# Loading r through GpSimd's queue from unit 8 on, in an RWKV-attention and squared-ReLU kernel with a planned order

## Chip, core and metric

The kernel runs on one core of one Trainium2 chip. The metric is device time in microseconds, of the whole launch. Before the change three runs gave a median of 180.85 us (178.78 to 181.63).

## What is computed

Two stages follow each other. The first is a linear attention with decay: per batch (4), head (8) and step (768), with head size 48,

```python
for t in range(S):
    cur = np.einsum('bhd,bhe->bhde', u[None] * kt, vt)
    y[:, :, t] = np.einsum('bhd,bhde->bhe', rt, state + cur)
    state = w[None, :, :, None] * state + np.einsum('bhd,bhe->bhde', kt, vt)
```

The second takes y as 3,072 tokens of 384 numbers and computes `relu(x @ w_in) ** 2 @ w_out`, with 2,048 numbers between the two products. Inputs and output are float32.

## The kernel before

**Units.** The sequence is cut into 6 chunks of 128 steps. A unit is one chunk of one batch with all 8 heads: 24 units, chunk by chunk, four batches in each. A unit has three loads of 192 KB, `rt`, `kt` and `vt` (`load`, L294); a row of such a load is one head of one step, 192 bytes long.

**Attention of a unit.** VectorE scales r and k by powers of w into `rkw` (L315). `rkw` is transposed into `rkT`: for the first six units on TensorE (L335) with evictions on ScalarE (L339), from then on by a DMA transpose (L324). TensorE multiplies the two halves of `rkT` (`at`, L352), VectorE applies the causal mask (L364) and multiplies the halves (`rk`, L344); `sums` (L372, L377) gives the diagonal term and the chunk's addition to the state; `dv` (L386) is VectorE's, the state is updated on VectorE (L394 to L400) and cast on ScalarE (L406). ScalarE casts v to `vb` (L319). `y` is summed on TensorE (L415 from the masked products, L421 from the state), `yb` is evicted on VectorE (L430), and turned into `xT` on TensorE for six units (L446), by a DMA transpose after that (L439).

**Second stage of a unit.** `mm1` (L462) multiplies with `w_in`, in four steps a unit, one for each quarter of `w_in`; the first eight units go alone (128 columns), the other sixteen in pairs (256 columns). ScalarE takes the ReLU out of PSUM (L470), and ScalarE (L477) or VectorE (L479) squares it into `g`, five to three. `mm2` (L486) multiplies `g` with the four quarters of `w_out` one after the other, `osb` is evicted on ScalarE (L493) and stored (L520). The last unit's second layer is cut in two column parts (L501, L510, L512, L516).

**Queues.** SyncE issues all loads, all stores and all DMA transposes, in its own program order. GpSimd issues the eight quarters of the weights (L303, L306), each after a one-element copy out of some unit's k (`gate`, L300), which keeps that weight behind this load. Both stand idle until what the next instruction on them waits for is there.

**The order.** Nothing is scheduled by the compiler: `Plan` holds every step with its engine, an estimated cost, what it needs, which buffers it takes and a rank, and `Plan.run` plays a list schedule through. Each engine takes the step with the lowest rank among those that are ready and whose buffers and PSUM banks are free; the order that comes out is the program order of that engine. For DMAs it keeps a model of each queue: at most about 1.5 us of work may be waiting, and queues that move at once share the rate. Fillers (`fill`, L262) are matmuls on a constant with the highest ranks, so they land in TensorE's planned waits, nearly all of them in the start.

Of the kernel before, what the change touches and what calls it, by code (L numbers as in the profile page):

```python
# [15 lines left out]

class Plan:

    def __init__(self, lags, cold):
        self.lags = lags
        self.cold = cold
        self.steps = []  # L30
        self.at = {}
        self.users = {}
        self.place = {}

    def add(self, key, engine, cost, emit, needs=(), rank=0.0, new=(), uses=(), move=None, cold=None):
        s = dict(key=key, engine=engine, cost=cost, emit=emit, rank=rank, new=new, move=move, cold=cold)
        s["needs"] = [n for n in needs if n is not None]
        self.at[key] = s
        self.steps.append(s)
        for x in tuple(new) + tuple(uses):  # L40
            self.users.setdefault(x, []).append(s)

    def run(self, room, banks, count):
        todo = {}
        for s in self.steps:
            todo.setdefault(s["engine"], []).append(s)
        for mine in todo.values():
            mine.sort(key=lambda s: s["rank"])
        rings = {name: [] for name in room}
        free = {e: 0.0 for e in todo}  # L50
        queues = {e: [] for e in todo}
        held = {n: None for n in range(count)}
        since = {n: 0.0 for n in range(count)}
        order = []
        t = 0.0
        left = len(self.steps)
        tiny = 1e-9

        moved, chained, left_pe, to_pe, near = self.lags

        def ready(s, e):
            if s["move"]:
                return s["end"] + moved
            if s["engine"] == "PE":
                return s["end"] + (chained if e == "PE" else left_pe)
            return s["end"] + (to_pe if e == "PE" else near)

        marks = []

        def mark(s):  # L70
            for e in ("PE", ""):
                heappush(marks, ready(s, e))

        def done(s, e):
            return "end" in s and ready(s, e) <= t + tiny

        def fits(s):
            e = s["engine"]
            names = [x[0] for x in s["new"]]
            for name in set(names):  # L80
# [3 lines left out]
                for n in range(len(ring) - m, len(ring) - m + names.count(name)):  # L84
                    if n >= 0 and not all(done(x, e) for x in self.users[ring[n]]):
                        return False
            wanted = [name for name in names if name in banks]
            if wanted:
                for n, x in held.items():
                    if x is not None and all(done(u, e) for u in self.users[x]):  # L90
                        held[n], since[n] = None, max(u["end"] for u in self.users[x])
                if sum(x is None for x in held.values()) < len(wanted):
                    return False
                for name in set(wanted):
                    mine = sum(x is not None and x[0] == name for x in held.values())
                    if mine + wanted.count(name) > banks[name]:
                        return False
            return True

        while left:  # L100
            for e, mine in todo.items():
                if free[e] > t + tiny:
                    continue
                for s in mine:
                    if s["move"] and sum(x[1] / x[0]["move"][0] * x[0]["move"][3] for x in queues[e]) > 1.5:
                        continue
                    if all(done(self.at[k], e) for k in s["needs"]) and fits(s):
                        mine.remove(s)
                        left -= 1
                        for x in s["new"]:  # L110
                            if x[0] in banks:
                                n = min((n for n in held if held[n] is None), key=lambda n: since[n])
                                held[n] = x
                                self.place[x] = n
# [4 lines left out]
                        if s["move"]:  # L119
                            queues[e].append([s, s["move"][0], free[e] + s["move"][2]])  # L120
                        else:
                            s["end"] = free[e]
                            mark(s)
                        order.append(s)
                        break
            heads = [q[0] for q in queues.values() if q]
            moving = [x for x in heads if x[2] <= t + tiny]
            whole = sum(x[0]["move"][1] for x in moving)
# [4 lines left out]
            later += [x[2] for x in heads if x[2] > t + tiny]  # L133
            later += [t + x[1] * whole / x[0]["move"][1] for x in moving]
            if not later:
                if left:
                    raise ValueError("nothing can go on: " + str([s["key"] for m in todo.values() for s in m[:3]]))
                break
            step = min(later) - t
            t += step  # L140
            for x in moving:
                x[1] -= step * x[0]["move"][1] / whole
                if x[1] <= 1e-7:
                    queues[x[0]["engine"]].pop(0)
                    x[0]["end"] = t
                    mark(x[0])
        return order
# [3 lines left out]
def kernel(  # L151
# [21 lines left out]
    NPE = 6  # L173
    NPY = 6
    NPAD = 5
    SQUARES = 'AMAMAAAM'
    GROUPS = (1,) * 8 + (2,) * 8
    PAIRED = ()

    const = ctx.enter_context(tc.tile_pool(name="const", bufs=1))  # L180
    loads = ctx.enter_context(tc.tile_pool(name="loads", bufs=6))
# [535 lines left out]
```

## Time and profile before

| what | value |
|---|---|
| three runs, median (lowest, highest) | 180.85 us (178.78, 181.63) |
| span of the profiled execution (clock granted 0.999) | 178.1 us |
| the profiled execution's own time beside its span | none is listed; the lowest run is 0.7 us over the span |
| TensorE busy | 169.5 us, of which fillers 12.5 |
| VectorE, ScalarE, GpSimd busy | 129.5, 128.4, 13.1 us |
| first `mm1`, last matmul's end | 15.1 us, 175.2 us |
| loads to landing, median: r, k, v | 3.6, 4.2, 4.1 us |
| stores; transposes rkT, xT; weights `w_in`, `w_out` | 2.4; 3.8, 3.0; 7.2, 10.1 us |

A row of a group gives line, engine, operation, tiles, the count, then the busy time, the mean in ns of one, the idle time before them and what ended most of it. Matmuls overlap in the pipeline, so TensorE's busy time is more than the sum of what each adds; what one adds is read from the chain of work that ended last, where pieces follow each other without overlap. A stretch's row gives its length and each engine's busy time in it.

### The profile page before, as it was taken

The page shows a single profiled execution, that of the slowest core. Times are in us where ns is not written, and L with a number is a line of the kernel's source. Part 1 is how long each engine was busy: PE and PEld are TensorE (multiplying, and loading weights), DVE is VectorE, ACT ScalarE, POOL GpSimd, SP SyncE. Part 2 cuts the span into 40 slices and gives each one's busy share as a digit, 9 for nine tenths or more (in the row PEclk, how much of TensorE's full clock was granted, in tenths as well). Part 3 has the DMA queues.
Part 4 walks back from the last instruction along what each step waited for, and adds up shares of the span by engine and source line. Part 5 has one row for each costly group of instructions (what it writes and reads, how often), then busy time and mean ns, then how long its engine had stood idle before and what let it go on. Part 6 is the DMA issues. An engine that isn't in the chain of part 4 may idle for free.

```text
span 178.1 us, 4985 instructions
## 1 busy us (share of the span) xinstructions
PE 169.5 (95%) x2013; PEld 134.9 (76%) x2013; DVE 129.5 (73%) x282; ACT 128.4 (72%) x266; POOL 13.1 (7%) x40
## 2 busy tenths in 40 slices
PE   7999799999999999999899899999999999999993
PEld 4778698987787786795696596786786885887972
DVE  4589697294999989689699598788798595771310
ACT  4556789999487984597598299498399494693941
POOL 6280650000000000000000000000000000000000
PEclk9999999999999999999999999999999999999999
DMA  6999899996595979879799999899999989953012
GB/s 115 188 182 204 156 198 199 207 184 109 84 207 118 184 140 171 175 152 207 159 175 192 155 180 151 189 178 141 200 201 151 192 184 161 262 177 110 0 48 88
DMA packets 107241, 28.84 MB, mean 162 GB/s; under 512 B 101969, under 2 KB 106706, under 8 KB 107218
## 3 DMA queue, kind: packets, MB, share of 16 engines
q1 hardware_dynamic: 104976, 25.37, 77.2%
q0 software_dynamic: 2240, 3.15, 9.8%
q8 instruction: 15, 0.25, 0.6%
q14 instruction: 8, 0.07, 0.1%
q10 hardware_dynamic: 2, 0.00, 0.0%
HBM read 20.45 MB, written 4.72 MB: 141 GB/s over the span
## 4 chain that ended last, share of the span: by engine, by line
PE 58%; DMA 21%; DVE 11%; ACT 4%; issue 1%; SPq 1%; POOL 1%; DVEq 0%; ACTq 0%
PE bank L462 26%; PE bank L486 20%; DMA rkT<-rkw 6%; DMA rt<-in_r_dram 5%; DMA w_in_q<-in_moe_w_in_dram 5%; PE bank L352 3%; DVE am L364 2%; DVE rkw L315 2%; DMA xT<-yb 2%; DVE g L479 2%; ACT gr L470 2%; DVE yb L430 2%; DMA vt<-in_v_dram 2%; PE bank L415 2%; PE bank L501 1%
## 5 line engine op out<-in xcount | busy, mean ns | idle before, releaser
L462 PE MATMUL bank<-xT,w_in_q 128*128 128x128 bf16 (+1 forms) x768 | 73.1, 246 | 2.0 <-DMA w_in_q<-in_moe_w_in_dram 1.3
L462 PEld LDWEIGHTS <-w_in_q 128*128 128x128 bf16 x768 | 62.4, 114 | 5.1 <-DMA w_in_q<-in_moe_w_in_dram 1.6
L486 PE MATMUL bank<-w_out_q,g 128*128 128x384 bf16 x368 | 64.7, 326 | 0.0
L470 ACT ACTIVATE gr<-bank 128x512 f32<-128x512 f32 x96 | 53.7, 594 | 10.3 <-PE bank L462 10.0
L486 PEld LDWEIGHTS <-g 128*128 128x128 bf16 x368 | 34.8, 98 | 20.2 <-DVE g L479 0.2
L479 DVE TENSOR_TENSOR g<-gr 128x512 bf16<-128x512 f32 x36 | 24.7, 687 | 19.5 <-ACT gr L470 19.5
L477 ACT ACTIVATE g<-gr 128x512 bf16<-128x512 f32 x60 | 37.0, 635 | 0.8
L364 DVE TENSOR_TENSOR am<-bank,smask 128x512 bf16<-128x512 f32 x48 | 31.6, 686 | 4.0 <-PE bank L352 3.6
L319 ACT CAST vb<-vt 128x384 bf16<-128x384 f32 x24 | 12.4, 515 | 15.4 <-DMA vt<-in_v_dram 15.3
L406 ACT CAST stb<-st 64x192 bf16<-64x192 f32 x40 | 14.0, 349 | 5.4 <-DVE st L400 4.3
L315 DVE TENSOR_TENSOR rkw<-kt,wneg 128x384 bf16<-128x384 f32 x24 | 13.3, 554 | 5.4 <-DMA kt<-in_k_dram 5.3
L315 DVE TENSOR_TENSOR rkw<-rt,wpos 128x384 bf16<-128x384 f32 x24 | 13.3, 552 | 3.8 <-ACT wpos L269 2.4
L430 DVE TENSOR_TENSOR yb<-bank,dv 128x384 bf16<-128x384 f32 x24 | 13.4, 557 | 2.3 <-PE bank L421 1.8
L493 ACT COPY osb<-bank 128x384 f32<-128x384 f32 x23 | 11.2, 486 | 5.3 <-PE bank L486 5.2
L344 DVE TENSOR_TENSOR rk<-rkT 128x512 bf16<-128x512 bf16 x24 | 10.1, 422 | 5.0 <-DMA rkT<-rkw 5.0
L262 PE MATMUL bank<-warm 128*128 128x128 bf16 x135 | 12.5, 244 | 1.1 <-DVE warm L209 1.1
L386 DVE TENSOR_TENSOR dv<-vb,bank 128x384 f32<-128x384 bf16 x24 | 13.1, 546 | 0.5 <-PE bank L377 0.4
L262 PEld LDWEIGHTS <-warm 128*128 128x128 bf16 x135 | 9.9, 111 | 2.3 <-issue 1.1
L396 DVE TENSOR_TENSOR st<-bank,st 64x192 f32<-64x192 f32 x32 | 11.3, 352 | 0.2
L352 PE MATMUL bank<-rkT 64*128 64x128 bf16 x192 | 9.7, 222 | 0.9 <-DMA rkT<-rkw 0.9
L352 PEld LDWEIGHTS <-rkT 64*128 64x128 bf16 x192 | 5.5, 95 | 6.4 <-issue 2.9
L415 PEld LDWEIGHTS <-am 128*128 128x128 bf16 x192 | 8.2, 96 | 1.9 <-DVE am L364 0.6
(57 smaller groups left out, 101.6 us busy)
## 6 DMA issues: line engine op xcount, KB each, us to landing
rt<-in_r_dram SPq DMA_DIRECT2D x24, 192.0 KB, 3.6
kt<-in_k_dram SPq DMA_DIRECT2D x24, 192.0 KB, 4.2
vt<-in_v_dram SPq DMA_DIRECT2D x24, 192.0 KB, 4.1
out_dram<-osb SPq DMA_DIRECT2D x23, 192.0 KB, 2.4
w_in_q<-in_moe_w_in_dram POOLq DMA_DIRECT2D x4, 384.0 KB, 7.2
w_out_q<-in_moe_w_out_dram POOLq DMA_DIRECT2D x4, 384.0 KB, 10.1
rkT<-rkw SPq DMA_TRANSPOSE x18, 3.8
xT<-yb SPq DMA_TRANSPOSE x18, 3.0
```

The lines of the kernel that those rows point to most:

```text
L262: nc.tensor.matmul(out=bank("fill")[:, :128], lhsT=warm, rhs=warm, start=True, stop=True)
L315: nc.vector.tensor_tensor(t["rkw"][:, x, :, :, :D], pair(src), pair(wx), ALU.mult)
L352: nc.tensor.matmul(out=t["at"][o][:, p, :], lhsT=t["rkT"][sl, 1, p, :], rhs=t["rkT"][sl, 0, p, :], start=True, stop=True,)
L364: nc.vector.tensor_tensor(am, t["at"][o], smask.unsqueeze(1).to_broadcast([C, HP, C]), ALU.mult)
L386: nc.vector.tensor_tensor(t["dv"], t["vb"], t["d"].unsqueeze(2).to_broadcast([C, H, D]), ALU.mult)
L406: nc.scalar.copy(stb[b][sl, :, o * D : (o + 1) * D], st32[b][sl])
L430: nc.vector.tensor_tensor(t["yb"], t["y"], t["dv"].rearrange("p h d -> p (h d)"), ALU.add)
L462: nc.tensor.matmul(out=t["h", s][:, a], lhsT=turned, rhs=chunks[c]["xT"][:, n, b : b + m, :], start=(n == 0), stop=(n == NK - 1),)
L470: nc.scalar.activation(t["gr", s], t["h", s], AF.Relu)
L477: nc.scalar.activation(g, x, AF.Square)
L479: nc.vector.tensor_tensor(g, x, x, ALU.mult)
L486: nc.tensor.matmul(out=t["o"], lhsT=chunks[units[i][0]]["g"][:, f, units[i][1], :], rhs=w_out_q[f // 4][:, f % 4, :], start=(f == 0), stop ...
```

## The change

r's loads from unit 8 on, and all stores but those of the last three units, are issued by GpSimd. k, v and the transposes stay on SyncE, and so does r of units 0 to 7. An r load on GpSimd needs, in the plan, that the r load three units earlier has landed.

All of the plan's settings move into one dictionary. The planner's DMA model is replaced: a move has a duration and a delay, two queues that move at once go at 0.62 each unless said otherwise, and instruction fetches are modelled as a stop of 2 us each time a count of planned PE instructions is passed (294 first, then every 246), in which GpSimd's queue goes at 0.85, SyncE's loads at 0.1 and its transposes not at all. Ranks of nearly all steps are new, and they can lie far from the unit's place.

Weights: the order by rank and the load that each is held behind are new. r, k and v get buffers of their own (4, 5, 4) in place of six of each, and other counts change too: rkT 3 for 4, vb 8 for 4, the masked products 6 for 4 each, yb 3 for 4, gr 10 for 8, osb 9 for 8, padded rkw tiles 4 for 5. The caps on PSUM banks by use rise (s 3, y 4, o 6), out of the same eight banks. The fillers are 68 of 256 columns in place of 135 of 128. Of eight squares, five stay on ScalarE in another pattern.

```diff
+P = {'squares': 'AAMAMAAM',
+ 'wide': 256,
+ 'fills': 68,
+ 'fetch': (294, 246, 2.0, (0.85, 0.0, 0.1)),
+ 'front': ('U0', 'U1', 'U2', 'U3', 'U4'),
+ 'weights': ('O0', 'I0', 'O1', 'O2', 'O3', 'I1', 'I2', 'I3'),
+ 'gates': {'I0': ('vt', 1), 'I1': ('kt', 3), 'I2': ('vt', 5), 'O0': ('vt', 3),
+           'I3': ('rt', 3), 'O1': ('kt', 4), 'O2': ('rt', 1), 'O3': ('rt', 2)},
+ 'rank': {'load': 72.19, 'vload': 7.28, 'scale': -0.67, 'rkT': 41.16, 'xT': 54.94, 'out': 43.52,
...
+ 'stores': 'POOL',
+ 'soft': ('rt',),
+ 'softfrom': 8,
+ 'depth': {'SP': 1.55},
...
     def load(i, name):
-        x = loads.tile([C, H, D], F32, name=name)
-        nc.sync.dma_start(
+        x = buffer({"rt": "ldr", "kt": "ldk", "vt": "ldv"}[name], [C, H, D], F32)
+        (nc.gpsimd if i >= P["softfrom"] and name in P["soft"] else nc.sync).dma_start(
...
-    def weights(i, q, which):
-        nc.gpsimd.tensor_copy(gate, tiles[i]["kt"][:, 0, :1])
+    def weights(after, q, which):
+        if after is not None:
+            nc.gpsimd.tensor_copy(gate, tiles[after[1]][after[0]][:, 0, :1])
...
-    def store(i):
-        nc.sync.dma_start(out=out[b * S + c * C : b * S + (c + 1) * C, :], in_=tiles[i]["osb"])
+    def store(i, where):
+        (nc.gpsimd if where == "POOL" else nc.sync).dma_start(out=..., in_=tiles[i]["osb"])
...
-    front = ['U0', 'U1', 'I0', 'I1', 'U2', 'U3', 'I2', 'O0', 'U4', 'I3', 'O1', 'O2', 'O3', 'U5']
...
+            hard = i < P["softfrom"] or name not in P["soft"]
             copy(
-                (name, i), SP, 0.55, do(load, i, name), rank=rank + 0.1 * n, move=(1.06, 16, 0.67, 1.0),
-                new=[("ld", i)] if n == 0 else (), uses=[("ld", i)] if n else (),
+                (name, i), SP if hard else POOL, 0.43 if hard else 1.2, do(load, i, name), rank=rank + 0.1 * n + (R["vload"] if n == 2 and i >= 6 else 0), move=moves["load"],
+                needs=[] if hard else [(name, i - 3)], new=[("ld" + name[0], i)],
             )
...
-                copy(("out", j), SP, 0.42, do(store, j), rank=a + 4 + L2, needs=[("osb", j)], move=(0.58, 75, 0.67, 0.13), uses=[("osb", j)])
+                where = P["stores"] if j < NU - 3 else SP
+                copy(
+                    ("out", j), where, 0.42 if where == SP else 0.7, do(store, j, where), rank=a + 4 + L2 + R["out"],
+                    needs=[("osb", j)], move=moves["out"], uses=[("osb", j)],
+                )
...
-    room = dict(
-        ld=6, rkw=NPAD, g=2, rkT=4, vb=4, rk=4, am=8, dv=4, yb=4, xT=3, gr=8, osb=8,
-    )
-    for s in plan.run(room, dict(at=4, s=2, y=2, h=5, o=2, fill=1), len(banks)):
+    for s in plan.run(P["room"], P["banks"], len(banks), P["depth"]):
```

More of the change, by code (lines that the diff above doesn't have):

```diff
@@ L39, in add, with run @@
         self.steps.append(s)
-        for x in tuple(new) + tuple(uses):
+        for x in s["new"] + s["uses"]:
             self.users.setdefault(x, []).append(s)
-    def run(self, room, banks, count):
+    def run(self, room, banks, count, depth, order=None):
+        tiny = 1e-9
         todo = {}
+        for s in order or self.steps:
+            todo.setdefault(s["engine"], []).append(s)
+            s.pop("end", None)
+            s["ready"] = None
+        if order is None:
+            for mine in todo.values():
+                mine.sort(key=lambda s: s["rank"])
@@ L68, in run, with end @@
[L68 to L78, printed above, removed]
+        first, every, stall, slow = self.fetch
+        fetched, frozen = 0, -1.0
+        marks = []
+        def end(s, at):
+            s["end"] = at
+            if s["move"]:
+                s["ready"] = (at + moved, at + moved)
+            elif s["engine"] == "PE":
+                s["ready"] = (at + chained, at + left_pe)
+            else:
+                s["ready"] = (at + to_pe, at + near)
+            for x in set(s["ready"]):
+                heappush(marks, x)
@@ L261, in fill @@
     def fill():
-        nc.tensor.matmul(out=bank("fill")[:, :128], lhsT=warm, rhs=warm, start=True, stop=True)
+        nc.tensor.matmul(out=bank("fill")[:, :WIDE], lhsT=warm[:, :128], rhs=warm, start=True, stop=True)
     def spread_log():
@@ L549 @@
[L549 to L559 removed]
+    add("wend", POOL, 2.6, end_columns, rank=P["wend"], needs=["copied"])
@@ L560 @@
+    place = {what: -100 + n for n, what in enumerate(P["front"])}
+    for n, what in enumerate(P["weights"]):
+        name, q = what[0], int(what[1])
+        held = P["gates"].get(what)
+        copy(
+            (name, q), POOL, 0.8 if held is None else 1.0, do(weights, held, q, name), rank=-99 + 0.01 * n, move=moves[name],
+            needs=[held],
+            uses=[("ld" + held[0][0], held[1])] if held else (),
+        )
     for i in range(NU):
```

356 lines of the change are left out of this document (220 added, 136 removed).

## Prediction

> **What bounds the kernel now.** I read five views of the profile of before, in this order: the page's first four parts, the engines' busy time by stretch, the chain of work that ended last, the issues of SyncE's queue, and the groups by line.
>
> The page first. TensorE is busy for 95% of the span, all loads, stores and transposes of the steady part are on one hardware queue (q1), the weights alone on GpSimd's (q0), and a small queue (q8) fetches instructions.
>
> ```profile
> PE 169.5 (95%) x2013; PEld 134.9 (76%) x2013; DVE 129.5 (73%) x282; ACT 128.4 (72%) x266; POOL 13.1 (7%) x40
> ...
> q1 hardware_dynamic: 104976, 25.37, 77.2%
> q0 software_dynamic: 2240, 3.15, 9.8%
> q8 instruction: 15, 0.25, 0.6%
> ...
> L262 PE MATMUL bank<-warm 128*128 128x128 bf16 x135 | 12.5, 244 | 1.1 <-DVE warm L209 1.1
> ```
>
> The 95% flatters: L262 is filler that keeps the clock up. Next the stretches, cut where each pair of units begins its long run of second-layer matmuls (columns: length, busy us and instructions of PE, PEld, DVE, ACT, POOL, then the granted clock, DMA share, GB/s).
>
> ```profile
> 0.00:31.60 31.60, 28.10 (x410) 24.08 (x411) 23.38 (x64) 21.74 (x43) 13.14 (x40) 1.00 1.09 178
> 31.60:67.80 36.20, 36.02 (x535) 29.25 (x534) 29.05 (x61) 30.56 (x66) 0.00 (x0) 1.00 0.81 152
> 67.80:81.50 13.70, 13.51 (x146) 10.44 (x144) 11.18 (x24) 9.10 (x19) 0.00 (x0) 1.00 0.86 175
> 81.50:94.70 13.20, 12.69 (x141) 9.82 (x138) 11.39 (x26) 9.73 (x21) 0.00 (x0) 1.00 0.88 177
> 94.70:108.30 13.60, 12.73 (x140) 9.89 (x138) 11.02 (x24) 9.82 (x22) 0.00 (x0) 1.00 0.99 177
> 108.30:121.20 12.90, 12.87 (x142) 9.90 (x139) 10.73 (x23) 9.74 (x22) 0.00 (x0) 1.00 1.02 172
> 121.20:134.20 13.00, 12.78 (x140) 9.94 (x138) 10.89 (x24) 9.45 (x21) 0.00 (x0) 1.00 1.03 178
> 134.20:146.90 12.70, 12.45 (x132) 9.49 (x129) 10.04 (x21) 9.92 (x23) 0.00 (x0) 1.00 1.04 177
> 146.90:158.60 11.70, 11.70 (x128) 9.20 (x126) 8.25 (x16) 7.98 (x17) 0.00 (x0) 1.00 1.03 228
> ```
>
> A pair's own work on TensorE, from the chain's pieces: 8 first-layer steps of 0.655, 8 second-layer quarters of 0.65, and twice the attention's matmuls (0.33 at L352, 0.08 and 0.19 at L372 and L377, 0.20 at L415, 0.17 at L421, some 1.05 with joints): 5.24 + 5.2 + 2.1 = 12.5 us. The six whole pairs took 13.7, 13.2, 13.6, 12.9, 13.0 and 12.7: 1.2 + 0.7 + 1.1 + 0.4 + 0.5 + 0.2 = 4.1 us lost. That is all that can be won there.
>
> Whole-kernel work by the same pieces: 21.4 (32 narrow steps of 0.667) + 41.9 (64 wide of 0.655) + 59.8 + 2.7 (second layer, last unit) + 8 + 6 + 8.5 + 4 (attention and transposes) is about 153 us. By 31.6 us only 13.8 of it is done (9 steps, 2 quarters, attention of four to five units): the start leaves 17.8 us unused. The end, from the last matmul at 175.2, takes 2.9. So 153 + 17.8 + 4.1 + 2.9, 177.8 of 178.1. The start, under DMA share 1.09, holds most of the slack.
>
> What causes the 4.1? The chain crosses the transposes of SyncE's queue in just those pairs:
>
> ```profile
> 83.04 3.95 DMA xT<-yb
> ...
> 94.09 5.96 DMA rkT<-rkw
> ...
> 120.67 5.38 DMA rkT<-rkw
> ```
>
> The median to landing of rkT is 3.8. The trace's packets of q8 start at 84.8, 98.2 and 123.2, inside these three. The stretches just before and at two such fetches, and then at one (30.4 us) with the weights on GpSimd's queue:
>
> ```profile
> 96.00:98.00 2.00, 2.00 (x14) 1.23 (x13) 1.72 (x4) 1.45 (x5) 0.00 (x0) 1.00 1.10 175
> 98.00:99.50 1.50, 1.41 (x9) 0.63 (x7) 0.00 (x0) 0.49 (x2) 0.00 (x0) 1.00 0.83 36
> ...
> 121.00:123.00 2.00, 2.00 (x22) 1.29 (x19) 1.96 (x6) 2.00 (x5) 0.00 (x0) 1.00 1.32 204
> 123.20:124.70 1.50, 1.50 (x11) 0.89 (x10) 0.66 (x2) 0.88 (x4) 0.00 (x0) 1.00 0.80 30
> ...
> 30.00:32.00 2.00, 2.00 (x25) 1.50 (x23) 0.98 (x2) 2.00 (x5) 0.00 (x0) 1.00 1.11 210
> ```
>
> The reader is to see 175 and 204 GB/s fall to 36 and 30 for 1.5 us, and 210 stand when the traffic is q0's. So a fetch all but stops q1, not q0. SyncE has no slack to make that up: from 81.05 to 94.09 its twelve issues take 11.34 of 13.04 us.
>
> **The change, part by part.**
>
> SyncE's queue. Per pair, two r loads (0.44 + 0.42) and two stores (0.57 + 0.53) go: 1.96 of the 11.34 us; 9.4 remain in 12.5. On q1, a load lands about 1.05 after the one before (rows of the start: 3.82, 4.95, 6.04, 7.08, 8.16), a store some 0.55 (155.02 to 158.61 in a row); 3.2 us of service a pair move to q0. k, v and both transposes remain, and so does each fetch's stop; but after it the queue has room, and the transposes have two fewer loads and two fewer stores ahead. I let 1.2 of the 4.1 remain: 0.2 for each of six fetches. Bounds: 4.1 gone, or none gone (the transposes still stop). Taken: −2.9.
>
> GpSimd's queue. Added: 16 r loads and 20 stores (the last three stay). The price of issuing r there has no row. The weights' issues took 0.78 us for 384 rows and 0.56 for 128, so 0.22 for 256 rows more; 1,024 rows extrapolate to 1.3, a store with 128 rows is 0.56. Bounds 0.56 and, by rows alone at 0.78 per 384, 2.1. Per unit 1.9 us of about 6.3, on an engine idle after 25 us: nothing on the path. Cover gone only if a store's wait for its osb holds an r behind it (rival 3).
>
> VectorE beside GpSimd's issuing: L364 averages 687 ns between 15 and 25 us, while the weights are issued, and 686 between 60 and 155; L479 692 and 686. At 1% that is at most 0.1 us of VectorE's 11 in a pair of 13, hidden: 0. The Trainium skill ("DMA: Bandwidth & Descriptors", SWDGE vs HWDGE vs iDMA) says that GpSimd writes its descriptors into SBUF, where VectorE's two-port modes lock it out. The only such candidate here may be L344, 0.42 us a unit; by the page an issue could be late by that much, which would not change the sum.
>
> The start. The weights get gates of their own and another order. In before they landed at 15.1 (I0), 19.1 (I1), 25.3 (I2), 27.4 (O0), 29.8 (I3), 32.5, 34.1 and 36.2. By the new gates (r1 for O2, v1 for I0, r2 for O3, r3 for I3, k3 for I1, v3 for O0, k4 for O1, v5 for I2) and r1's landing at 7.1, O2 goes ahead of I0; at about 2 us a weight I get I0 16.5, O3 18.5, I3 24, I1 26.5, O0 28.5, O1 30.5, I2 34. Until 16.5 TensorE has three units' attention (5.2), until 24 one quarter of three units and the fourth's attention (3.8), and from about 26 it always has work: unused 11.3 + 3.7 + 0.8, some 15.8 against 17.8. Taken: −2.0. Bounds −5 (TensorE fed from 24 on as if nothing were missing) and +3 (I2 a further unit late; nothing excludes it).
>
> The rest. Fillers: 68 of twice the width for 135; by the chain's 22 in 1.23 us, 135 × 0.056 = 7.6 and 68 × 0.112 = 7.6, in waits of the start: 0; put where no wait is, they cost what they last. Squares: 60 on ScalarE, 36 on VectorE as before. Two memsets of 0.11 fewer on VectorE. Buffers: four r and v tiles and five k for six of each; four units are 25 us of cover for a load that lands in 3.6; three rkT for four, at 12.5 a pair enough unless the order clusters two pairs. PSUM caps alone are wider. New ranks reorder all engines; VectorE's 11 of 13 us leaves least room there: 0, bounds ±2. Final stores stay on SyncE: 0.
>
> Sum: 178.1 − 2.9 − 2.0 = 173.2 of span. No time of the profiled execution stands beside its span; the fastest of the three runs is 178.78, 0.7 over it, the median 180.85, 2.7 over. With 2.7: 175.9 us against 180.85. Its own range, with the bounds partly together, is 171 to 177.2.
>
> **The rivals.**
>
> 1. The start pays (chance 0.15). O2 and O3 first move 4 us of weights that no matmul can use yet; I1 and I2 come later than now. For it: the start's DMA share 1.09, so whatever goes ahead delays the rest; against: the sum above. With +3 there and −2.9 later: 180.95.
>
> 2. The queue changes, the stalls stay (0.12): the transposes are as late behind each fetch, and the same 16 DMA engines carry it all. For it: DMA share about 1.03 from 108 to 147. Bulk 0, start −2: 178.85. The Trainium skill ("DMA: Bandwidth & Descriptors", Issuing engines are not separate DMA queues) says that DMAs of all issuers interleave on the same engines and that several issuers save issue time only. The trace disagrees in part: at 30.4 us q0 kept 210 GB/s where q1 fell to 36 and 30.
>
> 3. Slower (0.18): one in-order queue on GpSimd. A store waits for its osb, which waits for the fourth quarter of that unit's second layer; an r load issued behind it starts only then. Two units of second layer are 5.2 us, more than r's 3.6 to landing, and weights on that queue took 7.2 to 10.1. It decides where an r lands later than its turn at L315 by more than the 1.5 us that VectorE has free in a pair. Then the pair waits: eight pairs at 1.2 more than now is +9.6, less the start's 2.0: 188; at 0.8 a pair, 185. Against it: r is ranked far ahead, with four buffers.
>
> **How the numbers follow.** Forecast 0.55, rivals 0.15, 0.12 and 0.18. About 2% is what a measurement of this kernel can tell from no change, 177.2 to 184.5 here: rivals 1 and 2 fall inside, 3 beyond. So faster 0.55, same 0.27, slower 0.18. The range leaves out rival 3 and little of the forecast's low end: 170.5 to 184.
>
> **What would show it.** Queue part: q0 with 16 r loads and 20 stores, SyncE's issues near 9.4 us a pair; wrong if still over 11. Stalls: pairs near 12.7; wrong if they keep 13.2 and the chain still names rkT for 5 us and more. Issue price: r on GpSimd near 1.3 us. Start: I0 landing near 16.5, L486 steady by 30; wrong if filler at L262 or PE waits reach past 34 us. Rival 3 shows as VectorE waits at L315 for r. The forecast fails above all if the start is lost, the larger and less certain half.

## The result, and the profile after

The changed kernel takes 183.16 us (median of 20 runs, 181.03 to 185.48), the kernel before on the same chips 180.32 (20 runs, 178.64 to 182.02): a ratio of 1.0133, interval 1.010 to 1.0167. Ratios compare a kernel's fast runs alone, those within 1.5% of its fastest, so this one is below that of the medians; the profiled executions of e4, e6, e10 and e12 below were slower ones, so their profiles show too much loss, and e4, with one fast run, has no ratio. The change makes the kernel 1.3% slower, where 175.9 us had been forecast. That is clear of no change by its interval, and less than the 2% from which the prediction would call it slower. The profiled execution took 181.36 us around a span of 179.5, so 1.9 us lie outside the span.

First the page of the changed kernel. New line numbers: loads L384, scaling L406, transposition of `rkw` L415, `at` L443, mask L455, `sums` L463 and L468, `mm1` L553, `mm2` L577, fillers L352, stores L611.

```profile
span 179.5 us, 4854 instructions
...
PE 169.8 (95%) x1946; PEld 134.1 (75%) x1946; DVE 128.6 (72%) x280; ACT 133.0 (74%) x266; POOL 38.7 (22%) x77
...
q1 hardware_dynamic: 85312, 18.10, 66.9%
q0 software_dynamic: 4608, 10.43, 24.6%
q8 instruction: 15, 0.25, 0.6%
...
L611 POOL DMA_DIRECT2D out_dram<-osb x21 | 11.6, 552 | 98.6 <-ACT osb L584 98.6
...
L384 POOL DMA_DIRECT2D ldr<-in_r_dram x16 | 14.3, 897 | 6.4 <-DVE rkw L406 5.2
...
L352 PE MATMUL bank<-warm 128*128 128x256 bf16 x68 | 12.1, 322 | 1.2 <-DVE warm L299 1.2
```

TensorE's share is 95% as before and tells nothing. 7.3 MB have gone from q1 to q0, in 2,400 more packets there for 19,700 fewer on q1; an r load costs GpSimd 0.90 us to issue, a store 0.55. The busy time by stretch says where the span grew; first the changed kernel, then the kernel before in the two stretches that the prediction does not show.

```profile
0.00:31.60 31.60, 28.53 (x345) 22.76 (x346) 21.72 (x59) 21.80 (x45) 12.78 (x39) 1.00 1.09 189
31.60:67.80 36.20, 34.81 (x476) 26.60 (x473) 28.95 (x62) 26.89 (x56) 8.14 (x12) 1.00 1.10 185
67.80:100.00 32.20, 30.15 (x355) 24.13 (x354) 28.13 (x59) 24.78 (x53) 7.18 (x10) 1.00 1.22 183
100.00:158.60 58.60, 58.60 (x636) 46.90 (x634) 46.72 (x96) 47.65 (x95) 9.50 (x15) 1.00 0.84 158
```

```profile
67.80:100.00 32.20, 30.90 (x309) 22.90 (x306) 25.56 (x55) 22.07 (x47) 0.00 (x0) 1.00 0.89 170
100.00:158.60 58.60, 57.81 (x632) 45.79 (x633) 47.94 (x97) 43.68 (x92) 0.00 (x0) 1.00 1.03 190
```

TensorE is idle 1.4 us in the second stretch where it was idle 0.2 before, 2.1 in the third against 1.3, and not at all after 100 us against 0.8.

Busy time hides what pipelined matmuls add. So I counted, for each moment, the useful work finished by then at the prices of the prediction (0.667 and 0.655 us a first-layer step, 0.65 a second-layer quarter, and so on; 153.2 us in all) and call the moment less that work *lost*:

| us lost | by 40 us | 40 to 100 | 100 to 160 | after 160 | span |
|---|---|---|---|---|---|
| before | 16.2 | 2.9 | 2.9 | 2.9 | 178.1 |
| changed | 18.5 | 3.7 | 0.9 | 3.2 | 179.5 |

So the start costs 2.3 more, the steady part until 160 us 1.2 less, and the end 0.3 more. The chain of work that ended last names the places: 

```profile
14.01 9.38 DMA ldv<-in_v_dram
23.38 10.74 DMA ldr<-in_r_dram
...
34.15 0.56 DVE rkw L406
34.71 0.34 DVE rk L435
...
80.45 7.56 DMA ldv<-in_v_dram
...
89.95 6.24 DMA rkT<-rkw
```

And the waits of VectorE between 25 and 45 us, the longest first:

```profile
DVE rkw L406 <- DMA ldr<-in_r_dram: 5.4, 1, 5.4
```

r of unit 5, still a load of SyncE, is issued at 23.4 us and lands at 34.1; VectorE stands still for 5.4 us behind it, and TensorE then waits for its `rk`. In the kernel before this load was issued at 19.6 and VectorE never waited for r between 20 and 45 us. By 17 us the changed GpSimd has issued four weights, the one before two. At about 2 us a weight (the prediction's price) that is the 3.8 us by which unit 5's r starts later. Nothing else holds it: it is the sixteenth load of SyncE in both kernels, and the tile that it takes, with four for r in place of six, was free since VectorE had scaled unit 1's r at 7.8 us. Of the 2.3 us more by 40 us, 0.4 are lost by 34 us and the rest behind this wait.

### The profile page after: what moved, and what is told of

It is laid out like the page before. It is cut to its first block, busy times and chain, and to the rows that moved or that the text cites. A ratio compares the mean times of both kernels' runs of the same rounds, so it can differ in the third digit from the quotient of the medians.

```text
span 179.5 us, 4854 instructions
## 1 busy us (share of the span) xinstructions
PE 169.8 (95%) x1946; PEld 134.1 (75%) x1946; DVE 128.6 (72%) x280; ACT 133.0 (74%) x266; POOL 38.7 (22%) x77
## 4 chain that ended last, share of the span: by engine, by line
PE 61%; DMA 22%; SPq 7%; DVE 5%; ACT 2%; issue 1%
PE bank L577 27%; PE bank L553 24%; DMA ldv<-in_v_dram 9%; SPq L384 7%; DMA ldr<-in_r_dram 6%; DMA rkT<-rkw 3%; DMA xT<-yb 3%; PE bank L443 3%; PE bank L506 2%; DVE am L455 2%; PE bank L592 1%; PE bank L512 1%; PE bank L468 1%; PE bank L463 1%; ACT gr L561 1%
## 5 line engine op out<-in xcount | busy, mean ns | idle before, releaser
L553 PE MATMUL bank<-xT,w_in_q 128*128 128x128 bf16 (+1 forms) x768 | 75.2, 246 | 1.7 <-DMA w_in_q<-in_moe_w_in_dram 1.1
L553 PEld LDWEIGHTS <-w_in_q 128*128 128x128 bf16 x768 | 64.4, 114 | 8.4 <-DMA w_in_q<-in_moe_w_in_dram 1.3
L577 PE MATMUL bank<-w_out_q,g 128*128 128x384 bf16 x368 | 70.1, 326 | 0.0
L561 ACT ACTIVATE gr<-bank 128x512 f32<-128x512 f32 x96 | 55.6, 595 | 16.6 <-PE bank L553 15.4
L577 PEld LDWEIGHTS <-g 128*128 128x128 bf16 x368 | 34.1, 98 | 16.7
L455 DVE TENSOR_TENSOR am<-bank,smask 128x512 bf16<-128x512 f32 x48 | 31.6, 685 | 7.1 <-PE bank L443 6.3
L611 POOL DMA_DIRECT2D out_dram<-osb x21 | 11.6, 552 | 98.6 <-ACT osb L584 98.6
L406 DVE TENSOR_TENSOR rkw<-ldr,wpos 128x384 bf16<-128x384 f32 x24 | 13.2, 554 | 8.7 <-DMA ldr<-in_r_dram 6.2
L384 POOL DMA_DIRECT2D ldr<-in_r_dram x16 | 14.3, 897 | 6.4 <-DVE rkw L406 5.2
L584 ACT COPY osb<-bank 128x384 f32<-128x384 f32 x23 | 10.9, 475 | 6.0 <-PE bank L577 5.9
L406 DVE TENSOR_TENSOR rkw<-ldk,wneg 128x384 bf16<-128x384 f32 x24 | 13.3, 552 | 2.9 <-DMA ldk<-in_k_dram 2.8
L497 ACT CAST stb<-st 64x192 bf16<-64x192 f32 x40 | 13.9, 348 | 1.8 <-DVE st L491 1.4
L410 ACT CAST vb<-ldv 128x384 bf16<-128x384 f32 x24 | 12.2, 510 | 2.7 <-DMA ldv<-in_v_dram 2.5
L352 PE MATMUL bank<-warm 128*128 128x256 bf16 x68 | 12.1, 322 | 1.2 <-DVE warm L299 1.2
L430 ACT COPY rkT<-bank 128x512 bf16<-128x512 bf16 x12 | 7.0, 586 | 8.3 <-PE bank L426 8.3
L443 PE MATMUL bank<-rkT 64*128 64x128 bf16 x192 | 10.0, 226 | 1.3 <-DMA rkT<-rkw 1.1
```

Source lines behind the costliest of these rows:

```text
L384: (nc.gpsimd if i >= P["softfrom"] and name in P["soft"] else nc.sync).dma_start(out=x, in_=src[b, :, c * C : (c + 1) * C, :].rearrange("h ...
L406: nc.vector.tensor_tensor(t["rkw"][:, x, :, :, :D], pair(src), pair(wx), ALU.mult)
L443: nc.tensor.matmul(out=t["at"][o][:, p, :], lhsT=t["rkT"][sl, 1, p, :], rhs=t["rkT"][sl, 0, p, :], start=True, stop=True,)
L455: nc.vector.tensor_tensor(am, t["at"][o], smask.unsqueeze(1).to_broadcast([C, HP, C]), ALU.mult)
L497: nc.scalar.copy(stb[b][sl, :, o * D : (o + 1) * D], st32[b][sl])
L553: nc.tensor.matmul(out=t["h", s][:, a], lhsT=turned, rhs=chunks[c]["xT"][:, n, b : b + m, :], start=(n == 0), stop=(n == NK - 1),)
```

## The experiments

Ratios are to the kernel before on the same chip. *Met* counts the transpositions of `rkT` after 45 us in whose time from issue to landing an instruction fetch falls (from 1.5 us before the issue to 1 us before the landing).

| | ratio, interval | lost by 40 us | lost 40 to 160 us |
|---|---|---|---|
| e5 before, r moved | 1.0345, 1.0275 to 1.0414 | 15.6 | 11.1 |
| e6 before, stores moved | 1.003, 0.9993 to 1.0067 | 15.4 | 9.3 |
| e1 before, both | 1.0454, 1.0401 to 1.0508 | 15.7 | 13.1 |
| e7 before, r moved and held | 1.0107, 1.0043 to 1.0171 | 16.2 | 8.8 |
| e2 new plan, nothing moved | 1.0494, 1.0439 to 1.0549 | 19.2 | 11.0 |
| e3 new plan, stores moved | 1.0116, 1.0067 to 1.0166 | 19.0 | 5.0 |
| e4 changed order, r on SyncE | 184.76 us against 180.0, no interval | 19.0 | 7.7 |
| e8 new plan, old weights' order | 1.0512, 1.042 to 1.0604 | 15.9 | 13.9 |
| e9 changed, 68 fillers more | 1.0199, 1.0153 to 1.0245 | 18.4 | 5.3 |
| e11 changed, first r held | 1.022, 1.0166 to 1.0273 | 19.3 | 3.8 |
| e14 changed, two weights swapped | 1.0126, 1.0063 to 1.0188 | 18.1 | 6.5 |
| e15 before, 33 fillers fewer | 0.9963, 0.9932 to 0.9995 | 15.9 | 5.6 |
| e10 before, 67 fewer | 0.9882, 0.9835 to 0.993 | 16.6 | 4.6 |
| e16 before, 101 fewer | 0.987, 0.981 to 0.9931 | 15.2 | 5.5 |
| e17 before, 128 more | 1.0036, 0.9996 to 1.0076 | 16.4 | 7.3 |
| e12 before, r moved, 67 fewer | 1.0122, 1.0055 to 1.0189 | 16.3 | 10.9 |
| e13 before, stores moved, 67 fewer | 0.9932, 0.9894 to 0.9971 | 15.7 | 5.0 |

**The moves without the new plan: e1, e5, e6.** All engines keep the order of before; only the issuing engine of r from unit 8 on, and of the stores but those of the last three units, is changed.

```diff
-        nc.sync.dma_start(                                     # load
+        (nc.gpsimd if i >= 8 and name == "rt" else nc.sync).dma_start(     # e5, e1
-        nc.sync.dma_start(out=..., in_=tiles[i]["osb"])        # store
+        (nc.gpsimd if i < NU - 3 else nc.sync).dma_start(out=..., in_=tiles[i]["osb"])   # e6, e1
```

> The kernel before with its order on TensorE, VectorE and ScalarE untouched; only r from unit 8 on and all stores but the last three go out on GpSimd. Theory A (the moved queue relieves the steady part by some 2 us, and the changed kernel loses that and more in its start, between 30 and 40 us): 0.985 to 0.993 of before, that is 1.3 to 2.7 us faster, the idle of TensorE by 40 us unchanged at about 16, the pairs of units after 80 us shorter. Rival B (r and stores on GpSimd make k, v and the transposes late, so the move itself costs): 1.00 to 1.02, pairs no shorter, k and v at 4.4 us and more to landing. Rival C (GpSimd's in-order queue holds r behind stores): 1.03 and more, VectorE waits for r.

> The kernel before, order on TensorE, VectorE and ScalarE untouched, only r from unit 8 on moved to GpSimd; stores stay on SyncE. Theory E (collision: a moved r goes out the moment VectorE frees its buffer at L315, the moment in which SyncE also sends that unit's transposition; both share the DMA engines, and the transposition, on which everything waits, lands later): most of the 4.5% of the run with both moved, 1.03 to 1.045 of before, rkT at 5 us and more to landing. Rival G (the stores did it): 0.99 to 1.005.

> The kernel before, order untouched, only the stores but the last three moved to GpSimd. Theory E: a store has 0.55 us of service and meets a transposition by chance alone: 0.99 to 1.015, rkT near 4.2 to 4.5 us. Rival G: 1.03 to 1.045.

Moving r alone costs 3.4%, the stores nothing, both 4.5%. So the move by itself is a loss, and r makes it. Of the theories of e1, C has the number but not its sign: VectorE waits 0.7 us for r, but 14.1 us for `rkT` (5.0 in the kernel before). The waits of GpSimd in e1 and the chain of e5 show how:

```profile
POOL out_dram L520 <- ACT osb L493: 67.6, 19, 10.9
POOL rt L294 <- DVE rkw L315: 43.8, 8, 11.5
```

```profile
98.97 9.38 DMA rkT<-rkw
108.36 0.05 issue
108.41 0.40 PE bank L352 x8
```

An r load waits for a buffer, which VectorE frees with the scaling `rkw`; the same scaling releases the transposition on SyncE. So r and `rkT` start together and share the engines. By the issue and landing rows of e5, a transposition that meets neither a fetch nor q0 lands after 3.51 us (3 of them), one that meets q0 alone after 4.19 (6), one with a fetch alone after 4.80 (3), one with both after 6.31 (4); before, it was 3.50 without a fetch and 5.01 with one. The worst, above, took 9.38. Its stretches, in the columns of the prediction:

```profile
98.60:100.60 2.00, 2.00 (x14) 1.07 (x11) 0.73 (x2) 1.11 (x3) 0.89 (x1) 1.00 0.61 123
100.80:103.00 2.20, 2.20 (x32) 2.08 (x29) 1.91 (x4) 0.00 (x0) 0.00 (x0) 1.00 1.44 61
103.00:105.00 2.00, 1.44 (x22) 1.16 (x20) 0.46 (x2) 1.35 (x3) 0.00 (x0) 1.00 0.89 83
105.00:107.00 2.00, 0.00 (x0) 0.00 (x0) 0.00 (x0) 1.97 (x5) 0.00 (x0) 1.00 0.99 73
```

A fetch comes at 100.8. With r's rows on q0 neither queue keeps its rate: 61 to 83 GB/s for over six us, and TensorE does nothing at all from 105 to 107.

**The same collision taken away: e7.** r of unit j + 3 is issued on GpSimd only after unit j's `rkT` has landed.

```diff
+        if i < 9 or name != "rt":                                 # in load
+            load_now(i, name)
...
+        nc.gpsimd.tensor_copy(gate_b, t["rkT"][:, 1, HP - 1, C - 1 :])     # after the transposition of unit j
+        load_now(i + 3, "rt")
```

> As the run with r alone moved, but each r load (of the unit three further on, from unit 9) is held on GpSimd by a one-element copy out of rkT until the transposition just issued has landed, so that the two do not meet. Theory E: rkT back to 4.2 to 4.5 us to landing, 0.99 to 1.015 of before. Rival F (r's absence lets SyncE run into its own waits out of step, and whatever stands behind them is late): no better than with r alone moved, 1.03 and more.

Two thirds of the loss go, 1.0345 to 1.0107, with the same bytes on the same queue. So most of what r costs comes from when it starts. Of the rest, 2.5 us are one wait, again a fetch (87.6 us) on r and `rkT` together:

```profile
PE bank L360 <- DMA rkT<-rkw: 2.9, 2, 2.5
```

**The new plan without the moves: e2, e3, e4.** e2 and e3 take the changed planner with `soft` empty (and e2 the stores back on SyncE) and let it plan anew; e4 keeps the changed order of every engine but lets SyncE issue r, at r's place in the order.

```diff
- 'soft': ('rt',), 'stores': 'POOL',
+ 'soft': (), 'stores': 'SP',                    # e2; e3: 'soft' alone
-        (nc.gpsimd if i >= P["softfrom"] and name in P["soft"] else nc.sync).dma_start(
+        nc.sync.dma_start(                      # e4
```

> The changed kernel with r and the stores left on SyncE, and the order planned again with the same ranks, gates and buffers. Theory A: the start still loses some 2 us to before by 40 us, and the steady part loses what SyncE's queue costs: 1.02 to 1.04 of before. Rival B: without the moved transfers it is faster than the changed kernel, 1.00 to 1.01. Theory D (neither: new ranks alone cost in the steady part): 1.013 or more with the loss after 60 us.

> The changed kernel with r left on SyncE and the stores on GpSimd, planned again. Theory A: between the run with nothing moved and the changed kernel, 1.015 to 1.03 of before. Rival B (r's move costs, the stores' does not): faster than the changed kernel, 1.00 to 1.01.

> The changed kernel with the order of TensorE, VectorE and ScalarE untouched; only r from unit 8 on goes out on SyncE again, at the place in the program where it stood. Theory A: slower than the changed kernel by 1 to 4 us, 1.02 to 1.035 of before, with transposes landing later after 60 us. Rival B: faster than the changed kernel, 0.995 to 1.01 of before, with k and v landing earlier.

With the stores on GpSimd the new planner's kernel is 3.7% faster (e2 to e3), where in the old order they were worth nothing; with r there too it is no faster (1.0116 and 1.0133). Each of these has a plan of its own, so this is not the queue's worth alone: e8, with both moved, lies 3.7% over the changed kernel. e4 decides nothing: its six runs took 180.84 to 186.69 us, and the 7.7 us of steady loss (4.6 in the changed kernel) are those of an execution of 184.97. All three keep the loss of the start.

**The start: e8, e11, e14.** e8 gives the planner the weights' order and gates of before (and unit 5's loads among `front` again), and plans anew. e11 holds GpSimd's first r until unit 5's has landed, e14 exchanges two weights in GpSimd's program; both keep the order.

```diff
- 'weights': ('O0', 'I0', 'O1', 'O2', 'O3', 'I1', 'I2', 'I3'),
+ 'weights': ('I0', 'I1', 'I2', 'O0', 'I3', 'O1', 'O2', 'O3'),      # e8, with kt 1, 1, 3, 3, 4, 4, 4, 4 as gates
+        if i == 8 and name == "rt":                                # e11, in load
+            nc.gpsimd.tensor_copy(gate, tiles[5]["rt"][:, 0, :1])
+        which, q = {("O", 2): ("I", 1), ("I", 1): ("O", 2)}.get((which, q), (which, q))   # e14, in weights
```

> The changed kernel with the weights' order and gates of before (I0, I1 after k of unit 1; I2, O0 after k of unit 3; the rest after k of unit 4) and unit 5 loaded in front too; planned again. Theory A (the weights' new order costs the start its 2 to 3 us): TensorE's unused time by 40 us back from 18.5 to 16 to 16.8, the run 0.99 to 1.005 of before. Rival H (the start costs for another reason, as r of unit 8 ahead of r of unit 5): unused time stays at 18 and more, 1.01 and more.

> The changed kernel with one wait more: GpSimd takes a one-element copy out of unit 5's r before it issues the first r of its own (unit 8), so that this load, issued at 26.1 us in the changed kernel, starts after unit 5's has landed (34.2 us). Order and all else as in the changed kernel. Theory A (what is lost between 30 and 40 us is lost to traffic that goes ahead of unit 5's r, of which unit 8's load is a part of about 1 us of service): unit 5's r lands about 1 us earlier than the 10.7 us it took, unused time at 40 us falls from 18.5 to some 17.5, ratio to the kernel before 1.005 to 1.010. Rival B (weights O0 and O1, issued at 24.1 and 25.5, hold it back alone): it lands no earlier, ratio 1.011 to 1.018. If unit 8's r then comes late itself, VectorE waits for it and the ratio rises over 1.018.

> The changed kernel with its order untouched; only the places of two weights in GpSimd's program are exchanged: the second quarter of w_in goes first, behind unit 1's r, and the third quarter of w_out in its place behind unit 3's k. The latter is used only after the first two quarters of w_out, which land at 30.6 and 32.8 us, so nothing waits for it. Theory A (the start is lost because 4 us of weights that no matmul can use yet go first): TensorE's wait of 1.1 us at 27.4 us for that quarter goes, unused time at 40 us falls from 18.5 to 17.5 or less, ratio to the kernel before 1.004 to 1.010. Rival B (the start is lost to unit 5's loads, VectorE's wait of 5.4 us for its r, and the wait at 27.4 only anticipates it): unused time at 40 us stays within 0.4 of 18.5, ratio 1.011 to 1.017.

e8 has the old start back, 15.9 lost by 40 us, and so have all kernels with the order of before (15.2 to 16.6); every kernel with the new weights' order and gates, replanned or not, has 18.1 to 19.3. So the loss of the start comes with them. e8 loses more than it won later, though, in v's loads of a plan that came out otherwise:

```profile
78.30 6.14 DMA ldv<-in_v_dram
...
105.29 8.46 DMA ldv<-in_v_dram
```

Unit 5 among `front` moves no load up to its r, which is SyncE's sixteenth in e8 too (issued at 20.1 us). By which load the loss reaches TensorE is another question. e14 removes the wait for `w_in` at 27 us, and 18.1 are still lost, behind VectorE's wait for unit 5's r:

```profile
DVE rkw L407 <- DMA ldr<-in_r_dram: 5.1, 1, 5.1
```

That is rival B of e14. But e11 takes this wait away too. Unit 5's r lands 8.3 us after its issue and not 10.7, VectorE waits for it 0.4 us,

```profile
DVE rkw L408 <- DMA ldr<-in_r_dram: 0.4, 1, 0.4
```

and 19.3 us are lost by 40 us all the same, 19.0 of them by 31.6 us (16.3 in the changed kernel). Unit 3's k, which comes ahead of the edit, landed at 22.7 us in this execution and not at 20.8, and the quarter of `w_in` gated by it at 30.4 and not at 27.4. The ratio, 1.022, is above both theories of e11, and the late r of unit 8 that was to explain such a number is not there. e2, e3 and e4 are like e11: 18.2 to 18.6 us lost by 31.6 us and 0.3 to 0.9 more by 40, though VectorE waits 4.6 to 5.5 us for unit 5's r in them. The waits of TensorE and of VectorE in e2:

```profile
PE bank L553 <- DMA w_in_q<-in_moe_w_in_dram: 2.6, 1, 2.6
...
DVE rkw L406 <- DMA ldr<-in_r_dram: 5.5, 1, 5.5
```

So unit 5's r is where the loss shows in the changed kernel, and not its cause. What all these kernels share is that the loads of units 3 to 5 come later behind the weights: unit 3's k lands at 20.2 to 22.7 us (18.3 before, 19.5 in e8), unit 5's r is issued at 22.9 to 24.0 (19.6 and 20.1).

**Where the fetches fall: e9, e10, e15, e16, e17.** Fillers are halved, doubled or made four times as wide. Their columns stay about the same, but the number of matmuls ahead of the steady part does not, and the fetches, packets of 16 KB on q8, come every 124 matmuls or so on average (248 instructions with the weight loads; single intervals 81 to 176 in the kernel before). The Trainium skill ("Runtime: NRT & Kernel Launch", Instruction fetch mechanics) says that an engine's instruction memory is refilled in blocks of 256 instructions; the trace comes near it, with 248.

```diff
-        nc.tensor.matmul(out=bank("fill")[:, :128], lhsT=warm, rhs=warm, start=True, stop=True)
+        for n in [256] if count[0] % 2 == 0 else []:                # e10; e16: [512], one in four
+            nc.tensor.matmul(out=x[:, :n], lhsT=warm[:, :128], rhs=warm[:, :n], start=True, stop=True)
+        count[0] += 1                                               # e15: for 66 of 135; e17: [64, 64] for 128
```

> The changed kernel with its order untouched; only each of the 68 fillers of 256 columns is issued as two of 128, which take the same time on TensorE. So 68 more instructions lie ahead of the steady part, and as the fetches come at fixed counts of TensorE's instructions (about one in 120 matmuls, 10 to 13 us), each falls about half an interval earlier than where the planner had put it. Theory A (the order was laid around the fetches, and that is what the steady part gains: 0.9 us lost from 100 to 160 us against 2.9 before): the fetches now meet transposes that stood clear of them, two us or more are lost again, 1.01 to 1.02 of the changed kernel, 1.02 to 1.035 of the kernel before. Rival B (the emptier queue of SyncE alone makes the steady part better, wherever the fetches fall): within 0.5 us of the changed kernel, 1.010 to 1.017 of the kernel before.

> The counterpart on the kernel before: its 135 fillers of 128 columns become 68 of 256, nothing else changes, so 67 fewer instructions lie ahead and each fetch falls about half an interval later. Its planner knew nothing of fetches, so by theory A (where the fetches fall decides about one to two us) the time may go either way, by up to 2 us: beyond 0.995 to 1.005. By rival B (places do not matter) it stays within 0.995 to 1.005.

> The kernel before; of its 135 fillers 66 become 33 of twice the width, so 33 matmuls fewer lie ahead of the steady part and each fetch falls about a quarter of an interval (some 3 us) later; with 67 fewer it took 0.988. Theory A (where the fetches fall decides a per cent or so): the ratio is another one for each shift, and goes with the number of rkT transpositions that a fetch meets (8 of 17 before, 1 of 17 with 67 fewer), here between, 0.985 to 1.005. Rival B (fewer, wider fillers are cheaper by themselves, wherever the fetches fall): about half of the gain, 0.991 to 0.997, and with 101 fewer more than the whole, under 0.988.

> The kernel before with 34 fillers of 512 columns in place of 135 of 128: 101 matmuls fewer, fetches later by some four fifths of an interval of about 124 matmuls, so nearly back where they were before. Theory A: most of the gain of 67 fewer (0.988) is given back, 0.993 to 1.005. Rival B (wider fillers are cheaper by themselves): under 0.988. The memset of the constant is some tenths longer before the first filler, in a stretch where nothing else is ready: 0.

> The kernel before with 128 of its 135 fillers issued as two of 64 columns: 128 matmuls more, one whole interval between fetches, so each fetch but the first falls where another one fell before. Theory A: the same time as before, 0.995 to 1.005, with the fetches in the steady part within 2 us of their places. Rival B (narrow fillers cost, wide ones save): slower by as much as 67 fewer won or more, over 1.008.

Nothing is done to a queue in any of these. Of 17 transpositions, a fetch meets 8 in the kernel before, 6 with 33 fillers fewer, 1 with 67, 3 with 101, and 8 again with 128 more, a whole interval. The ratios go 1, 0.996, 0.988, 0.987, 1.004. They also follow the number of fillers, so they alone do not rule out that fewer fillers are cheaper; but at most 2 of the fillers in any of these kernels come after 31.6 us, and e10 wins its time after 40 us (4.6 us lost from 40 to 160 us against 5.8 before; by 40 us it is 16.6 against 16.2). The median of `rkT` (the issues to landing; 3.8 in the kernel before) in e10 and e17:

```profile
rkT<-rkw SPq DMA_TRANSPOSE x18, 3.6
```

```profile
rkT<-rkw SPq DMA_TRANSPOSE x18, 4.1
```

The chain's shares by line say it too, e10 first, then e17: `rkT` holds 2% of the one and 9% of the other.

```profile
PE bank L466 27%; PE bank L490 25%; DMA rt<-in_r_dram 7%; DMA w_in_q<-in_moe_w_in_dram 5%; ACT gr L474 4%; DMA vt<-in_v_dram 3%; PE bank L356 3%; DMA rkT<-rkw 2%; PE bank L419 2%; DVE rkw L319 2%; SPq L298 2%; PE bank L505 1%; PE bank L425 1%; PE bank L381 1%; PE bank L265 1%
```

```profile
PE bank L466 22%; PE bank L490 12%; DMA rkT<-rkw 9%; DMA vt<-in_v_dram 7%; DMA rt<-in_r_dram 4%; DMA w_in_q<-in_moe_w_in_dram 4%; DVE rkw L319 4%; DVE g L483 3%; ACT gr L474 3%; DVE am L368 3%; DVE yb L434 2%; DMA kt<-in_k_dram 2%; SPq L298 2%; PE bank L356 2%; PE bank L505 1%
```

e15 fits both theories. In e17 the way back with a whole interval speaks against the fillers' width (rival B of e17 wanted over 1.008), though its fetches come back only to within 4 us of the old places (64.6 for 64.0, 102.0 for 98.2 us). One expectation failed: e16 was to give most of the gain back, and came out as its rival B said, under 0.988. It meets 3 transpositions and not 8, but a full us of its gain lies in the start (15.2 lost by 40 us), which fetch places in the steady part do not explain; there fewer and wider fillers may be what helps. In the changed kernel the shift goes the other way (e9): the 0.9 us lost from 100 to 160 us become 2.6, but the 3.7 until 100 become 2.8, and 0.7% are added, a little under what theory A gave. A fetch meets 6 transpositions and not 7, so their number does not explain it, and the intervals of e9 and of the changed kernel overlap: e9 does not decide.

e10 and e16 are the fastest of all kernels here, with not one DMA moved.

**Moves and fetch places together: e12, e13.** e5 and e6 with the fillers of e10.

> The kernel before, its order untouched, with r from unit 8 on issued by GpSimd (alone that cost 3.4%) and its 135 fillers issued as 68 of twice the width, so that the fetches come later by half an interval (alone that won 1.2%). Theory A (the loss from moving r is made where a fetch meets r and rkT on both queues; between fetches the two queues share without loss that matters): with the fetches elsewhere most of it goes, 0.99 to 1.01 of the kernel before. Rival B (r on a second queue makes every transposition later, 4.2 instead of 3.5 us without any fetch, and that alone starves TensorE): the two effects add, 1.015 to 1.03.

> The kernel before, its order untouched, with all stores but the last three units' on GpSimd (alone 1.003) and the 68 wide fillers (alone 0.988). If the two add: 0.985 to 0.995. If stores in a second queue help a transposition past a fetch, which in this placing they would meet more often (six stores fall on a fetch, one transposition of rkT): under 0.985. If they lengthen the transpositions everywhere as r did: over 0.995.

Against e10 (0.9882), r moved is 2.4% slower (1.0122/0.9882), where it was 3.4% in the old places: most of the loss of e5 does not hang on its places. Whether some does is not shown; the ratio lies between the ranges of the two theories, and its interval reaches into both. In e12, 7 transpositions that meet q0 and no fetch took 4.75 us, against 3.54 of 6 without either. The stores are again worth nothing (0.9932/0.9882 = 1.005), though beside them, too, transpositions land later: 4.01 us in e13 (12 that meet q0 and no fetch) against 3.63 in e10.

## Why the prediction was wrong, point by point

**The start, −2.0: measured +2.3 by 40 us.** This is the step that decided. I0's landing (16.5 predicted, 18.2 measured) and "from about 26 it always has work" failed; 0.3 more than before are lost by 31.6 us and 2.0 between there and 40. What the working left out is the other queue: the two weights ahead of I0 and I3 do not only come early themselves, they push back SyncE's loads of units 3 to 5, on which VectorE and the weights' gates, each in order, then stop. Rival 1 had this ("whatever goes ahead delays the rest"), and +3 was the prediction's own upper bound. That the new weights' order and gates make the loss is shown by e8 against all the others; by which load it reaches TensorE differs (unit 5's r in the changed kernel and e14, unit 3's k in e2, e3, e4 and e11), and this part is read from waits and landings, not from an edit.

**The queue part, −2.9: measured −1.2 between 40 and 160 us**, made of +0.8 until 100 and −2.0 after. SyncE's issues fell as said (per pair 2 × (0.79 + 0.61 + 1.55 + 1.38) = 8.7 us, 9.4 predicted), and it bought little, since the transposes did not land earlier for it. The premise "a fetch all but stops q1, not q0" was read at the two hardest of nine fetches (between 50 and 150 us of the kernel before, 30 to 98 GB/s in the 1.5 us behind seven of them, 184 and 197 behind two), and for q0 at one place with weights, in the start; it does not hold for r's rows (e5). In the changed kernel's own fetches at 82.6 and 94.2 us:

```profile
80.50:82.50 2.00, 2.00 (x39) 1.83 (x36) 2.00 (x5) 2.00 (x6) 0.88 (x1) 1.00 1.03 220
82.50:84.00 1.50, 1.50 (x17) 1.43 (x14) 1.50 (x4) 1.46 (x5) 0.00 (x0) 1.00 2.28 84
92.10:94.10 2.00, 2.00 (x31) 1.99 (x29) 1.92 (x5) 2.00 (x5) 0.00 (x0) 1.00 1.22 177
94.10:95.60 1.50, 1.01 (x16) 0.74 (x14) 1.50 (x3) 1.50 (x4) 0.00 (x0) 1.00 1.52 119
...
83.00:85.00 2.00, 2.00 (x17) 1.55 (x16) 2.00 (x4) 1.96 (x6) 0.00 (x0) 1.00 1.28 27
```

220 falls to 84 and 177 to 119, and behind the first fetch all queues together move 27 GB/s for 2 us. By the trace's packets q0 moves nothing from 83 to 85 us, though an r load issued at 80.5 us lands only at 87.8: q0 is no free lane. And "fewer loads ahead" has a price that the sum had at nothing: a transposition that no fetch meets took 3.50 us before and 4.00 in the changed kernel (3.21 in e2, from the same planner with nothing moved), one that meets a fetch 5.01 and 5.24. Rival 2 had this right: the Trainium skill ("DMA: Bandwidth & Descriptors", Issuing engines are not separate DMA queues) says that issuers share the same engines and that a second one saves issue time only; for r, e5 and e12 agree with the page and overrule my objection. Moreover e10 wins the same 1.2 us (5.8 to 4.6) with nothing moved, so the gain that is left can't be credited to the queue.

**Ranks at 0, bounds ±2 us.** Too narrow for this planner: e2 and e8 are plans of it and lie 9 us over the kernel before. What the ranks do in the changed kernel itself no run takes apart.

**Fillers at 0.** Right for their columns, wrong for their number: it sets where the fetches fall, and the kernel before gains 1.2% by 67 fewer (e10).

**Right:** a store's issue (0.56 predicted, 0.55); r's issue in its bounds (1.3, measured 0.90); VectorE unharmed beside GpSimd's issuing (L455 685 ns, before 686), and no issue of r held up by 0.42 us (0.88 to 0.92 us, all 16); the final stores. Rival 3 did not happen: VectorE waits 6.2 us for r in all, 5.4 of them for SyncE's load in the start.

**The median over the span, +2.7:** the profiled execution shows 1.9.

The sum as measured: 178.1 + 2.3 − 1.2 + 0.3 = 179.5. The medians differ by 2.8 us where the spans differ by 1.4, because the profiled execution of the changed kernel (181.36 us) is the second lowest of its 20 runs: a usual run of it loses one to two us more than this sum, and where is not shown. Open is also how much of the changed kernel's good stretch after 100 us its planner's model of fetches earns and how much is chance; e9, one shift with overlapping intervals, can't say.

## What to carry to other kernels

A transfer on another issuer's queue is not out of the way: ask which event releases it, and which urgent transfer the same event releases, and hold the lazy one until the urgent one has landed. In a start limited by transfers, price every weight by the loads that it pushes back, on whatever queue they are. And before crediting 1% to a change, shift the instruction stream by a few dozen instructions that compute nothing needed and time it again.

## What the runs showed of the hardware

- The instruction fetches come at about the same counts of TensorE's instructions in both orders (every 124 matmuls on average, 10 to 13 us in the steady part). Behind seven of the nine between 50 and 150 us in the kernel before, the data queues moved 30 to 98 GB/s for 1.5 us, and transpositions that met one took 5.01 us against 3.50. With nothing but the number and width of the fillers changed, the kernel before took 0.987 to 1.004 of its time.
- The same r load lands later from GpSimd's queue: median 4.5 us there in e5 and 5.3 in the changed kernel, against 3.6 from SyncE's before. On q0 r travels in packets of 3,840 and 4,224 bytes, 20 and 22 rows together (shortest 149 and 161 ns), on q1 row by row (192 bytes, 13 ns). A transposition's packets have 256 bytes (15 ns). That they stand behind r's large ones on an engine would explain their delay; it was not tried apart.
